# Block 0 of layer one in fp32, and weights converted in pieces of twice the width: a Trainium2 attention and two-layer kernel

## The chip, the core and the metric

The kernel runs on one core of a Trainium2 chip. The metric is device time in microseconds (us) of one execution. The core's engines work side by side, each through its own instructions in a fixed order: TensorE (PE) multiplies, VectorE (DVE) and ScalarE (ACT) work element by element, SyncE (SP) issues DMA transfers, GpSimd (POOL) does little here. An instruction starts when the semaphores that it waits for allow it; what stands behind it on its engine waits too.

## The reference

Three stages follow each other. The inputs q, k, v, M_prev, z_prev, beta and the first layer's w_in are drawn eight times larger than the drawing functions show.

```python
# B, H, S, D = 4, 8, 576, 64
scores = where(causal, -1e9, q @ k.T / sqrt(D))
a = exp(scores - max); a /= sum + 1e-9
local = a @ v
q_p = phi(q)                              # elu(q) + 1
mem = (q_p @ M_prev) / (q_p . z_prev + 1e-6)
x = g * mem + (1 - g) * local             # g = sigmoid(beta); x is 2304 x 512
h = x @ moe_w_in;  x = softplus(h) @ moe_w_out      # 512 -> 2048 -> 512
h = x @ moe2_w_in; out = relu(h) ** 2 @ moe2_w_out  # 512 -> 2048 -> 512
```

The weights arrive as 64-bit floats.

## The kernel before

**Attention** goes through 18 groups of 128 rows; nine blocks of 256 rows (two groups each) are what the layers work on. A step is one head or a few heads of a group: scores on PE, the masked maximum on DVE (line 315), the exponential on ACT (319), a split of P into two fp16 parts (331, 332), its transposition by DMA on SP (196), the product with V (355), and at a group's half and end the normalisation (374, 381) and the split and transposition of x (385 to 387). The first two groups are transposed on PE and copied by ACT (203).

**Numbers.** A product of nearly fp32 accuracy is made of three 16-bit products: each factor is split into a high and a low part, and high x high, high x low and low x high are added. In layer one these are lines 434 to 436 (h, 256 columns), 451 to 453 (output x) and 496 to 498 (the same, accumulated by quarters).

**Weights.** A piece of the first layer's weights, 128 x 4 x 128 elements of 64 bits (512 KB), is loaded through SP into one of three staging buffers (`wst`, lines 398 and 401). DVE turns its bits into fp32 with three operations (417 to 419), ACT copies the high part (421), DVE subtracts for the low part (422). There are 32 pieces: 16 of W1, 16 of W2.

**Layer one** consists of units: `h` (two of 16 column chunks of a block, then softplus on ACT, 438 to 440, DVE 441, and the split of g, ACT 444 and DVE 445), `x` (half the output columns of a block) and, for block 0, `xq` (a quarter of the sum over 2048, accumulated in PSUM over all of `xq`'s four calls). The second layer follows when all attention is done.

**Order.** A planner written out in Python emits attention steps and, between them, the units of a queue. Up to the step that completes block 0's input, W1R pieces of weights are emitted for each step. From there the queue holds, four times: eight pieces, two `h` units, one `xq` unit. FR says what share of the queue's estimated time is spread over the steps that complete block 1. A scheduler then orders each engine's instructions by emission and by priority: attention's scores have 100, weight conversions 2000 (`HW`), so conversions are taken long before their place in the emission. At `kb == 1` a passage interleaves an early part of block 1 (lines 649 to 668).

Of the kernel before, what the change touches and what calls it, by code (L numbers as in the profile page):

```python
# [8 lines left out]
F32 = mybir.dt.float32  # L9
F16 = mybir.dt.float16  # L10
# [7 lines left out]
P = 128  # L18
# [3 lines left out]
FR = 0.4  # L22
W1R = 1
B1Q = 3
# [14 lines left out]
NST = 3  # L39
# [6 lines left out]
ST2 = 4  # L46


@with_exitstack
def kernel(  # L50
# [61 lines left out]
    W1 = [w1p.tile([P, NCC, DFF], t, name=f"W1{i}") for i, t in enumerate((F16, BF16))]  # L112
    W2 = [w1p.tile([P, NFC, DM], t, name=f"W2{i}") for i, t in enumerate((F16, BF16))]
# [28 lines left out]
    make_identity(nc, ident)  # L142
    dve.memset(zero, 0.0)
# [222 lines left out]
    def emit_x(g, a):  # L366
# [15 lines left out]
        if a == 0:  # L382
            return
        xn = att.tile([P, 2, H, D], F16, name="xn")
# [21 lines left out]

    def split_piece(i, t, Ws, pool_):
# [7 lines left out]
        w = t.bitcast(I32).rearrange("p (n two) -> p n two", two=2)  # L415
        u = pool_.tile([P, 512], I32, tag="wcv", name="wcv", bufs=WCB)
# [6 lines left out]

    g_t = {}

    def unit_h(kb, fp):
        ps = mm.tile([P, 2, NB], F32, tag="mm", name="hps")
        x = x_at(kb)
        for i in range(2):
# [10 lines left out]
        act.activation(a, a, AF.Ln, bias=one[:, 0:1])  # L440
        dve.scalar_tensor_tensor(a, ps, 0.0, a, ALU.max, ALU.add)  # L441
        g = [w1p.tile([P, 2, NB], F16, name=f"g{t}_{fp}") for t in range(2)]
# [4 lines left out]
    def mm_x(ps, kb, c, f0, f1):  # L447
        for f in range(f0, f1):
            gh, gl = (t[:, f % 2] for t in g_t[kb, f // 2])
            wh, wl = (w[:, f, c * P:(c + 1) * P] for w in W2)  # L450
# [34 lines left out]
    def unit_xq(kb, q):  # L485
        if q == 0:
            for i in range(2):
                t = xac.tile([P, 2, 256], F32, name=f"xacc{i}")
                pe.matmul(t, zero, g_t[kb, 0][0], start=True, stop=False)
                xacc.append(t)  # L490
        for c in range(NCC):
            ps = xacc[c // 2][:, c % 2]
            for f in range(4 * q, 4 * q + 4):
                gh, gl = (t[:, f % 2] for t in g_t[kb, f // 2])
                wh, wl = (w[:, f, c * P:(c + 1) * P] for w in W2)
# [20 lines left out]
    order = [i for a in range(4) for i in [4 * a + t for t in range(4)] + [NPC + 4 * t + a for t in range(4)]]  # L516
# [487 lines left out]
```

## Time and profile before

| | |
|---|---|
| median of 3 runs | 960.42 us (958.69 to 961.71) |
| the profiled execution's own time | 961.28 us |
| its span in the trace | 959.5 us |
| PE busy | 878.4 us, 92% |
| DVE busy | 738.2 us, 77% |
| ACT busy | 615.6 us, 64% |

Busy PE is taken from matmul records whose ends are modelled and overlap, so it isn't PE at its peak. [...]

### The profile page before, as it was taken

What the parts mean: (1) busy time and instruction counts of PE and PEld (TensorE: products, weight loads), DVE (VectorE), ACT (ScalarE), POOL (GpSimd) and SP (SyncE); (2) the same over time, 40 slices, a digit from 0 to 9 for tenths busy, and PEclk for the clock granted to TensorE, in tenths of its full rate; (3) what the DMA queues carried; (4) which work ended last, traced back from release to release, by engine and by line L of the source; (5) the groups of instructions that cost most, each with busy time, mean ns of one, the idle gap of its engine ahead of it and who ended that gap; (6) DMA issues with size and microseconds to landing.
All of it is one profiled execution on the core that took longest, in us unless ns stands there. A gap on an engine that the chain in (4) does not pass through costs nothing.

```text
span 959.5 us, 24660 instructions
## 1 busy us (share of the span) xinstructions
PE 878.4 (92%) x10372; PEld 729.9 (76%) x10380; DVE 738.2 (77%) x1490; ACT 615.6 (64%) x1144; POOL 2.2 (0%) x10
## 2 busy tenths in 40 slices
PE   4436799899999899999999999999999999999998
PEld 3225688788878788898887888544595999999993
DVE  7997999777747766586846589999999998867640
ACT  8865878778758787796947547563357655544630
POOL 0000000000000000000000000000000000000000
PEclk8555899999999999999999999999999999999999
DMA  9999978677679996767754385630000000000001
GB/s 236 220 244 215 233 158 154 114 119 104 111 109 175 171 155 100 111 109 126 112 82 85 49 250 158 197 107 12 33 3 23 2 23 2 24 24 2 24 13 33
DMA packets 285024, 101.25 MB, mean 106 GB/s; under 512 B 248048, under 2 KB 284400, under 8 KB 284912
## 3 DMA queue, kind: packets, MB, share of 16 engines
q1 hardware_dynamic: 284672, 99.65, 53.1%
q8 instruction: 81, 1.33, 0.6%
q14 instruction: 31, 0.25, 0.1%
q10 hardware_dynamic: 240, 0.02, 0.0%
HBM read 48.78 MB, written 4.72 MB: 56 GB/s over the span
## 4 chain that ended last, share of the span: by engine, by line
PE 60%; DMA 16%; DVE 12%; ACT 6%; issue 3%; SPq 1%; DVEq 0%; ACTq 0%
DMA PT<-p 9%; PE h2ps L811 5%; PE h2ps L809 5%; PE h2ps L810 5%; PE ops L870 3%; PE ops L869 3%; PE ops L871 3%; PE hps L435 3%; PE hps L436 3%; PE hps L434 3%; PE s_ps L310 3%; DMA rawv<-in_v_dram 3%; PE pvt L355 3%; PE xps L452 2%; PE xps L453 2%
## 5 line engine op out<-in xcount | busy, mean ns | idle before, releaser
L434 PE MATMUL hps<-x,W 128*128 128x256 f16 x576 | 158.1, 276 | 3.0 <-DVE cc L276 2.2
L436 PE MATMUL hps<-x,W 128*128 128x256 f16 x576 | 158.6, 276 | 0.0
L435 PE MATMUL hps<-x,W 128*128 128x256 f16 x576 | 158.5, 276 | 0.1
L452 PE MATMUL xps<-g,W 128*128 128x256 f16 x512 | 139.3, 274 | 1.8 <-DVE g L445 1.7
L451 PE MATMUL xps<-g,W 128*128 128x256 f16 x512 | 138.2, 274 | 1.5 <-ACT g L444 1.4
L453 PE MATMUL xps<-g,W 128*128 128x256 f16 x512 | 139.3, 274 | 0.0
L319 ACT ACTIVATE Pt<-Pt,cs 128x128 f32<-128x128 f32 (+4 forms) x144 | 84.1, 584 | 51.9 <-DVE cs L315 51.6
L310 PE MATMUL s_ps<-KT,qT 128*128 128x128 f16 (+2 forms) x992 | 82.5, 225 | 31.2 <-DVE cs L315 30.7
L332 DVE TENSOR_TENSOR p<-Pt,p 128x512 f16<-128x512 f32 (+2 forms) x104 | 69.3, 666 | 34.4 <-ACT p L331 34.1
L310 PEld LDWEIGHTS <-qT 128*128 128x128 f16 (+1 forms) x992 | 58.3, 105 | 42.7 <-issue 37.5
L315 DVE CUSTOM_DVE_ANT_0 Pt<-s_ps,mask 128x128 f32<-128x128 f32 (+3 forms) x128 | 62.0, 484 | 22.8 <-PE s_ps L310 22.7
L355 PE MATMUL pvt<-V,PT 128*128 128x64 f16 (+1 forms) x1392 | 60.0, 197 | 16.6 <-DMA PT<-p 15.0
L355 PEld LDWEIGHTS <-PT 128*128 128x128 f16 (+1 forms) x1392 | 50.2, 104 | 25.9 <-DMA PT<-p 22.0
L331 ACT ACTIVATE p<-Pt 128x512 f16<-128x512 f32 (+2 forms) x104 | 63.1, 606 | 10.6 <-DMA PT<-p 9.4
L435 PEld LDWEIGHTS <-W 128*128 128x128 f16 x576 | 57.0, 99 | 10.1 <-issue 3.4
L436 PEld LDWEIGHTS <-W 128*128 128x128 bf16 x576 | 56.9, 99 | 7.1 <-issue 0.2
L434 PEld LDWEIGHTS <-W 128*128 128x128 f16 x576 | 57.0, 99 | 6.8
L421 ACT ACTIVATE W<-wcv 128x512 f16<-128x512 f32 x64 | 40.0, 625 | 30.6 <-DVE wcv L419 30.3
L453 PEld LDWEIGHTS <-W 128*128 128x128 bf16 x512 | 50.4, 98 | 8.2 <-issue 2.5
L445 DVE TENSOR_TENSOR g<-spa,g 128x512 f16<-128x512 f32 x72 | 49.4, 686 | 9.1 <-ACT g L444 8.7
L451 PEld LDWEIGHTS <-W 128*128 128x128 f16 x512 | 50.3, 98 | 7.6 <-issue 1.7
L441 DVE SCALAR_TENSOR_TENSOR spa<-hps,spa 128x512 f32<-128x512 f32 x72 | 49.4, 686 | 8.3 <-ACT spa L440 7.9
(230 smaller groups left out, 2554.6 us busy)
## 6 DMA issues: line engine op xcount, KB each, us to landing
wst<-in_moe_w_in_dram SPq DMA_DIRECT2D x32, 512.0 KB, 4.5
wst<-in_moe_w_out_dram SPq DMA_DIRECT2D x32, 512.0 KB, 4.6
rawk<-in_k_dram SPq DMA_DIRECT2D x16, 256.0 KB, 4.7
rawq<-in_q_dram SPq DMA_DIRECT2D x16, 256.0 KB, 4.5
rawv<-in_v_dram SPq DMA_DIRECT2D x16, 256.0 KB, 4.7
out_dram<-T SPq DMA_DIRECT2D x12, 256.0 KB, 2.5
PT<-p SPq DMA_TRANSPOSE x100, 3.4
mraw<-in_M_prev_dram SPq DMA_DIRECT2D x8, 128.0 KB, 4.1
```

What stands on the lines that cost most here:

```text
L310: pe.matmul(o[x * n:(x + 1) * n], qT[g][:, t * H + h, x * n:(x + 1) * n], KT[kb][:, h, a - j * P:e - j * P], start=(t == 0), stop=(t == 1),)
L315: dve.tensor_tensor_reduce(out=pw, in0=view, in1=mw, scale=-0.125, scalar=3.0e38, op0=ALU.add, op1=ALU.min, accum_out=cs[:, 0, h:h + 1],)
L319: act.activation(pf, pf, AF.Exp, bias=cs[:, 0, h:h + 1], scale=-1.0, accum_out=cs[:, 1, h:h + 1],)
L331: act.activation(v16[:, :, 0], p, AF.Copy)
L332: dve.tensor_tensor(v16[:, :, 1], p, v16[:, :, 0], ALU.subtract)
L355: pe.matmul(o[r], t[:, o0 + i + y, r], V[kb][:, z, h, :], start=(i == 0 and y + z == 0), stop=(i == nb - 1 and y > 0),)
L434: pe.matmul(o, wh, x[:, c], start=(c == 0), stop=False)
L435: pe.matmul(o, wh, x[:, NCC + c], start=False, stop=False)
L436: pe.matmul(o, wl, x[:, c], start=False, stop=(c == NCC - 1))
L451: pe.matmul(ps, wh, gh, start=(f == f0), stop=False)
L452: pe.matmul(ps, wh, gl, start=False, stop=False)
L453: pe.matmul(ps, wl, gh, start=False, stop=(f == f1 - 1))
```

## The change

Block 0 goes through layer one with fp32 operands and one product where three 16-bit ones were. Its input is transposed as fp32 on PE and copied once; its g stays fp32. The weights come in 16 pairs of pieces (1 MB, rows of 2 KB), through two staging buffers in place of three. The three bit operations write fp32 weights into slot n + 1 of one tile; after block 0's units of a group are emitted, a new unit `c` forms the high and low part of pair n in slot n, over the fp32 weights of the pair before. Block 1 accumulates by quarters as block 0 does, and the passage for its early part is gone. FR goes from 0.4 to 0.7, W1R from 1 piece to half a pair for a step. The second layer's weights keep their path.

```diff
-FR = 0.4
-W1R = 1
+FR = 0.7
+W1R = 0.5
...
-NST = 3
+NST = 2
...
+NF = 1
+HC = 0
...
-    W1 = [w1p.tile([P, NCC, DFF], t, name=f"W1{i}") for i, t in enumerate((F16, BF16))]
-    W2 = [w1p.tile([P, NFC, DM], t, name=f"W2{i}") for i, t in enumerate((F16, BF16))]
+
+    slots = w1p.tile([P, NFC + 1, 1024], F32, name="W12")
...
+        if kb < NF:
+            ps = mm.tile([P, NCC, P], F32, tag="mm", name="tps")
+            xf = xf.rearrange("p h d -> p (h d)")
+            for c in range(NCC):
+                pe.transpose(ps[:, c], xf[:, c * P:(c + 1) * P], ident32)
+            act.activation(x2_at(kb)[:, off // P::2], ps, AF.Copy)
+            return
         xn = att.tile([P, 2, H, D], F16, name="xn")
...
+    def load_pair(i):
+        t = stage.tile([P, 1024], I64, name="wst")
+        o = t.rearrange("p (a b) -> p a b", a=4)
+        if i < NPC // 2:
+            src = moe_w_in[:, 2 * i * P:2 * (i + 1) * P].rearrange("(c p) f -> p c f", p=P)
...
+        sp.dma_start(out=o, in_=src)
+        return t
...
+    def slot32(n):
+        n, o = divmod(n, 2)
+        return slots[:, n + 1].rearrange("p (a b) -> p a b", a=4)[:, :, o * P:(o + 1) * P]
+
+    def split_slot(n):
+        u = slots[:, n + 1]
+        t = slots[:, n].bitcast(F16).rearrange("p (t a) -> p t a", t=2)
+        hi, lo = t[:, 0], t[:, 1].bitcast(BF16)
+        act.activation(hi, u, AF.Copy)
+        dve.tensor_tensor(lo, u, hi, ALU.subtract)
...
             for c in range(NCC):
-                wh, wl = (w[:, c, f * P:(f + 1) * P] for w in W1)
+                if kb < NF:
+                    pe.matmul(
+                        o.rearrange("p (j t) -> p j t", j=2), slot32(pos[f])[:, c], x32[:, 2 * c:2 * c + 2],
+                        start=(c == 0), stop=(c == NCC - 1),
+                    )
+                    continue
+                wh, wl = (w[:, c] for w in slot(pos[f]))
...
+        if kb < NF:
+            g_t[kb, fp] = w1p.tile([P, 2, NB], F32, name=f"g0_{fp}")
+            dve.scalar_tensor_tensor(g_t[kb, fp], ps, 0.0, a, ALU.max, ALU.add)
+            return
...
+                if kb < NF:
+                    m = pe.matmul(
+                        ps, slot32(n)[:, f % 4], g_t[kb, f // 2][:, f % 2],
+                        start=False, stop=(f == NFC - 1 and c % 2 == 1),
+                    )
+                    continue
...
-            return 1700.0 if u[0] == "w" else 0.0
-        nmm = {"h": 24, "xq": 48, "x": 96 if len(u) == 3 else 48}[u[0]]
+        if u[0] in ("w", "c", "close"):
+            return {"w": 3000.0, "c": 0.0, "close": 0.0}[u[0]]
+        nmm = {"h": 24 if u[1] >= NF else 32, "xq": 48 if u[1] >= NF else 64, "x": 96 if len(u) == 3 else 48}[u[0]]
...
+        elif u[0] == "c":
+            with tc.high_priority(HC):
+                split_slot(u[1])
...
             with tc.high_priority(HW):
-                split_piece(order[i], pieces.pop(i), (W1, W2), stage)
-            if i + NST < 2 * NPC:
-                pieces[i + NST] = load_piece(order[i + NST], (moe_w_in, moe_w_out), sp, stage)
+                bits(pieces.pop(i), slots[:, i + 1].bitcast(I32))
+            if i + NST < NPC:
+                pieces[i + NST] = load_pair(order[i + NST])
...
-        queue += [("w", i) for i in range(max(nw, 8 * a), 8 * a + 8)]
+        queue += [("w", i) for i in range(max(nw, 4 * a), 4 * a + 4)]
         queue += [("h", 0, f) for f in range(2 * a, 2 * a + 2)] + [("xq", 0, a)]
+        if NF == 1:
+            queue += [("c", i) for i in range(4 * a, 4 * a + 4)]
...
+            for a in range(4):
+                queue += new[2 * a:2 * a + 2] + [("xq", 1, a)]
+                queue += [("c", i) for i in range(4 * a, 4 * a + 4) if NF == 2]
+            queue.append(("close",))
+            continue
```

## Rows read from the trace of the kernel before

**Rows 1.** The page's busy line, and two lines of its 40 slices.
```profile
PE 878.4 (92%) x10372; PEld 729.9 (76%) x10380; DVE 738.2 (77%) x1490; ACT 615.6 (64%) x1144; POOL 2.2 (0%) x10
...
PE   4436799899999899999999999999999999999998
...
PEclk8555899999999999999999999999999999999999
```
**Rows 2.** Windows: stretch, length, busy PE, PEld, DVE, ACT, POOL, clock, DMA share, GB/s.
```profile
11.00:85.00 74.00, 32.36 (x349) 24.26 (x344) 69.81 (x181) 55.28 (x126) 0.00 (x0) 0.54 1.15 235
85.00:120.00 35.00, 29.03 (x305) 23.58 (x306) 29.68 (x70) 24.64 (x49) 0.00 (x0) 0.79 1.14 231
120.00:185.00 65.00, 63.27 (x749) 57.22 (x748) 57.67 (x130) 49.56 (x104) 0.00 (x0) 1.00 0.73 142
185.00:222.00 37.00, 31.15 (x410) 27.24 (x408) 27.95 (x60) 28.06 (x57) 0.00 (x0) 0.95 0.78 120
222.00:300.00 78.00, 75.35 (x1127) 64.54 (x1125) 50.80 (x109) 58.84 (x118) 0.00 (x0) 1.00 0.76 122
```
**Rows 3.** Timeline of DVE: start and duration in us, then the instruction.
```profile
40.82 0.68 DVE L418 SCALAR_TENSOR_TENSOR wcv<-wst,wcv 128x512 int32<-128x512 int32 x1
41.42 0.68 DVE L221 TENSOR_TENSOR qn<-rawq,qn 128x512 f16<-128x512 f32 x1
42.02 0.42 DVE L417 TENSOR_SCALAR wcv<-wst 128x512 int32<-128x512 int32 x1
42.36 0.28 DVE L315 CUSTOM_DVE_ANT_0 Pt<-s_ps,mask 128x128 f32<-128x128 f32 x1
```
**Rows 4.** Windows of line 422 (two rows), then of line 417 (one).
```profile
11.00:84.20 73.20, 10.28 (x15) 0.55 1.15 236
84.20:185.00 100.80, 11.55 (x17) 0.92 0.87 173
...
11.00:84.20 73.20, 6.74 (x16) 0.55 1.15 236
```
**Rows 5.** Chain of work, 83 to 100 us; instructions of tile hps, first and last start.
```profile
84.25 0.68 DVE xn L386
...
L434 PE MATMUL hps<-x,W x576: 269/273/421, 87.2 to 583.9; 128*128 128x256 f16 x192
```
**Rows 6.** Windows of tile hps in a full stretch: PE, DVE, ACT.
```profile
563.00:584.00 21.00, 20.75 (x191) 3.41 (x5) 3.57 (x6) 1.00 0.60 182
```
**Rows 7.** PE's groups by line and shape, 87 to 222 us.
```profile
L434 PE MATMUL hps<-x,W 128*128 128x256 f16 x144 | 41.2, 286 | 3.0 <-DVE cc L276 2.2 <-ACT x L203 0.8
...
L498 PE MATMUL xacc<-g,W 128*128 128x256 f16 x64 | 18.6, 293 | 0.0
...
L453 PE MATMUL xps<-g,W 128*128 128x256 f16 x64 | 17.2, 273 | 0.0
...
L310 PE MATMUL s_ps<-KT,qT 128*128 128x128 f16 x184 | 16.0, 224 | 1.1 <-DVE cs L315 1.1
L355 PE MATMUL pvt<-V,PT 128*128 128x64 f16 x312 | 14.4, 195 | 7.9 <-DMA PT<-p 7.9
L347 PE MATMUL pvt<-Mt,phiT 128*128 128x64 f16 x72 | 8.1, 195 | 0.0
```
**Rows 8.** Timeline of SP's DMA queue: start, duration of the issue.
```profile
65.78 0.51 SPq L401 DMA_DIRECT2D wst<-in_moe_w_out_dram  x1
66.81 0.37 SPq L180 DMA_DIRECT2D rawq<-in_q_dram  x1
...
67.91 4.01 SPq L196 DMA_TRANSPOSE KT<-kn  x1
```
**Rows 9.** Waits, 85 to 222 us: total us, times, longest us.
```profile
PE pvt L355 <- DMA PT<-p: 7.9, 6, 2.5
ACT spa L438 <- PE hps L436: 7.6, 5, 2.9
```
**Rows 10.** A line of the page's costliest groups: PE's weight loads.
```profile
L453 PEld LDWEIGHTS <-W 128*128 128x128 bf16 x512 | 50.4, 98 | 8.2 <-issue 2.5
```

More of the change, by code (lines that the diff above doesn't have):

```diff
@@ L142 @@
     make_identity(nc, ident)
+    ident32 = stage.tile([P, P], F32, name="ident32", bufs=1)
+    make_identity(nc, ident32)
     dve.memset(zero, 0.0)
@@ L440, in unit_h @@
         act.activation(a, a, AF.Ln, bias=one[:, 0:1])
+        if kb < NF:
+            g_t[kb, fp] = w1p.tile([P, 2, NB], F32, name=f"g0_{fp}")
+            dve.scalar_tensor_tensor(g_t[kb, fp], ps, 0.0, a, ALU.max, ALU.add)
+            return
         dve.scalar_tensor_tensor(a, ps, 0.0, a, ALU.max, ALU.add)
-        g = [w1p.tile([P, 2, NB], F16, name=f"g{t}_{fp}") for t in range(2)]
+        t = w1p.tile([P, 2, NB], F32, name=f"g0_{fp}")
+        t = t.rearrange("p a b -> p (a b)").bitcast(F16).rearrange("p (t a b) -> p t a b", t=2, a=2)
+        g = [t[:, 0], t[:, 1]]
         g_t[kb, fp] = g
@@ L448, in mm_x @@
         for f in range(f0, f1):
+            n = pos[NPC + 4 * c + f // 4]
+            if kb < NF:
+                pe.matmul(ps, slot32(n)[:, f % 4], g_t[kb, f // 2][:, f % 2], start=(f == f0), stop=(f == f1 - 1))
+                continue
             gh, gl = (t[:, f % 2] for t in g_t[kb, f // 2])
-            wh, wl = (w[:, f, c * P:(c + 1) * P] for w in W2)
+            wh, wl = (w[:, f % 4] for w in slot(n))
             pe.matmul(ps, wh, gh, start=(f == f0), stop=False)
@@ L488, in unit_xq @@
                 t = xac.tile([P, 2, 256], F32, name=f"xacc{i}")
-                pe.matmul(t, zero, g_t[kb, 0][0], start=True, stop=False)
-                xacc.append(t)
+                pe.matmul(t, zero, mask[:, 0], start=True, stop=False)
+                xacc[i:i + 1] = [t]
         for c in range(NCC):
@@ L515 @@
     pieces = {}
-    order = [i for a in range(4) for i in [4 * a + t for t in range(4)] + [NPC + 4 * t + a for t in range(4)]]
+    order = [i for a in range(4) for i in [2 * a + t for t in range(2)] + [NPC // 2 + 4 * t + a for t in range(2)]]
+    for n, i in enumerate(order):
+        for o in range(2):
+            c, g = divmod(i - NPC // 2, 4)
+            pos[2 * i + o if i < NPC // 2 else NPC + 4 * (2 * c + o) + g] = 2 * n + o
     steps = [(g, h) for g in range(NC) for h in range(0, H, GRP[g])]
@@ L544 @@
     for i in range(NST):
-        pieces[i] = load_piece(order[i], (moe_w_in, moe_w_out), sp, stage)
+        pieces[i] = load_pair(order[i])
     prep_m(0)
@@ L619 @@
         s += 1
-        while nw < 2 * NPC and nw < W1R * s:
+        while nw < NPC and nw < W1R * s:
             run_unit(("w", nw))
@@ L648 @@
         if kb == 1:
-            done = 4 - sum(u[0] == "xq" for u in queue)
-            if done < 4:
-                at = 0
-                while done < B1Q:
-                    done += queue[at][0] == "xq"
-                    at += 1
-                nh = 2 * done
-                early = new[:nh] + [("x", kb, c, 0, 2 * nh) for c in range(NCC // 2)]
-                out_q = queue[:at]
-                for u in queue[at:]:
-                    if u[0] != "w" and early:
-                        out_q += early
-                        early = []
-                    out_q.append(u)
-                    if u[0] == "w" and early:
-                        out_q.append(early.pop(0))
-                queue = out_q + early + [("close",)]
-                if done < 4:
-                    new = new[nh:]
-                    xs = [("x", kb, c, 2 * nh, NFC) for c in range(NCC // 2)]
-            else:
-                queue.append(("close",))
+            for a in range(4):
+                queue += new[2 * a:2 * a + 2] + [("xq", 1, a)]
+                queue += [("c", i) for i in range(4 * a, 4 * a + 4) if NF == 2]
+            queue.append(("close",))
+            continue
         queue += new + xs
```

24 lines of the change are left out of this document (18 added, 6 removed).

## The prediction

> **What bounds the kernel now.** I read the page's busy line first: PE is busy 92% of the span, so what PE does not do in time is lost. The slices then say where it is not busy: its digits are 3 to 7 in the first five slices (120 us), and the granted clock is half in the second to fourth [rows 1]. The windows give the same in microseconds [rows 2]: from 11 to 85 us DVE is busy 69.8 of 74 us and PE 32.4, at a granted clock of 0.54; from 120 us on PE is busy 63.3 of 65, while DVE is still at 57.7; from 185 to 222 PE sinks to 31.2 of 37; later it is full. So the start is bound by DVE, the rest by PE, and the 961.28 us are PE's work plus what PE misses, most of it before 120 us.
>
> How fast DVE really goes is seen in its timeline, not in durations: neighbouring starts [rows 3] lie 0.60 us apart for a 512-wide fp32 or int32 operation of two inputs (40.82 to 41.42) and 0.34 us for the one-input shift (42.02 to 42.36), though they last 0.68 and 0.42. A weight piece costs DVE 0.34 + 3 x 0.60 = 2.14 us. Up to 84.2 us 16 pieces were begun and 15 ended [rows 4]: 16 x 1.54 + 15 x 0.60 = 34 us of DVE. The last DVE step of block 0's input is at 84.25 us, its first product of layer one at 87.2 us [rows 5].
>
> How much PE has to do: in a full stretch at full clock 191 products of 256 columns took 21 us [rows 6], 0.11 us each; I scale with columns (0.055 for 128, 0.027 for 64). From 87 to 222 us, about when block 1 has left layer one, there are 144 products on each of three h lines and 64 on each of three lines for block 0's and again for block 1's second half, together 816 of 256 columns, 184 of 128, 384 of 64 and a few tiny ones [rows 7]: 89.8 + 10.1 + 10.4 + 2 = 112 us of work in 135 us. PE misses 23 us there.
>
> **The change, part by part.** The sum is made against the profiled execution, 961.28 us, which lies 0.86 above the median of 960.42; the span is 959.5 and 1.8 lie around it.
>
> (1) Work taken from DVE before block 0 is ready. The subtraction for the second part of the weights goes behind block 0: 15 x 0.60 = 9.0 us. The two input splits of block 0 go: 1.2 us. Pieces twice as wide: a start-to-start time of 0.60 is 512 columns and a rest; the shift's 0.34 at the same rest fits 0.27 + 0.07, so 0.07 is saved for each operation merged, 0.2 us for each pair, 1.6 us for eight pairs. Together 11.8 us. From above, then, block 0 is ready 12 us earlier; from below not at all, or somewhat later, since nothing but two staging buffers holds the conversions back. I take 8, two thirds, because DVE was 94% busy there and SP is nearly as full: its DMA instructions of 57 to 72 us follow each other almost without a gap, transposes taking up to 4.0 us [rows 8], and halving the number of weight loads frees only about 0.5 us each, eight times. What is next late is those transposes and loads.
>
> [...]
>
> (2) PE's added work. Block 0 loses 384 products of 0.11 us (42.2 us) and gets 128 in fp32. No row of this kernel shows an fp32 product. From below: it costs what one 256-column product costs, 128 x 0.11 = 14 us, a gain of 28. From above: twice four of them (four at the half clock that this stretch partly has), 113 us, a loss of 70. I take four, 0.44 us: a factor with twice the digits is two halves, two such factors make four products of halves, and the kernel's own scheme leaves out the fourth. That is 56.3 us, +14. The eight opening and input transposes for block 0 become eight fp32 ones, under 1 us either way.
>
> [...]
>
> (3) What PE misses between block 0's start and 222 us. Before, a group of eight pieces asks 8 x 2.14 = 17.1 us of DVE for 96 products, 10.6 us of PE: block 0 waits for DVE. After, the group's four pairs ask 4 x 2.87 = 11.5 us of DVE for 32 fp32 products, 14 us of PE: DVE can feed it. Its total work in the stretch hardly changes: 17 pieces [rows 4] at 2.14 were 36.4 us; eight pairs of bits at 2.87 and 16 wide subtractions at 1.13 are 41.1, less eight g subtractions and two additions of partial sums (10 x 0.60). PE's work is 126 us against some 113 of DVE. Bounds: all 23 us are recovered, or none. PE's largest wait there is for the transposes of P, 7.9 us in six waits [rows 9], and it stays. I take 10.
>
> (4) Added waits. Each split of a pair writes over the fp32 weights of the pair ahead, so the copy on ACT waits for block 0's products on them. Queued behind it on ACT are the exponentials of later attention steps and the next softplus; DVE's p split and PE's score products wait for those. In emission order the splits stand behind the unit that they wait for, so I price this at 0, covered by PE's distance from ACT; without that cover it is the second rival. Block 1's first accumulation must wait until block 0's sums have left PSUM (four operations of about 0.6 us, 2.4 us); two h units of block 1 (48 products, 5 us) stand between, and if they don't cover it the scores behind it on PE wait those 2.4 us. The first two loads are 1 MB instead of three of 512 KB; M's second load is queued behind them on SP, 0.5 MB later, about 2 us at the 235 GB/s of that stretch [rows 2], and not needed before block 0's second step. ACT loses eight g copies and merges 32 weight copies to 16; it is not the bound (55.3 of 74 us).
>
> (5) FR and W1R shift units against attention steps; total work is unchanged, and their worth is in (1) and (3).
>
> Sum: 961.28 - 8 + 14 - 10 = 957.3, and 0.86 less for the median: 956.5 us. Nothing behind 222 us changes.
>
> **Rivals.**
> A, the start gives more: the full 11.8 us, and PE misses only 6 us of the 23. 961.28 - 12 + 14 - 17 - 0.86 = 945.5. For it: DVE at 94%. Against: SP's fullness.
>
> B, slower: the early places that DVE gets free are filled by conversions. They have priority 2000, and the two staging buffers hold four pieces' worth where three held three. From three more pairs (8.6 us) ahead of block 0's input the gain of (1) is gone; PE's 14 us stay, and 4 of (3) come back: 961.28 + 14 - 4 - 0.86 = 970.5. For it: 16 pieces had been begun by 84 us [rows 4], twice the eight that the emission order has put out by the step that completes block 0's input. Against: a pair holds its buffer longer (1 MB to land, 2.87 us of DVE where 1.54 was), so by 75 us again about eight pairs are through.
>
> C, slower: the copies of the splits stand too early in ACT's order and ACT waits for fp32 products. Four groups; a wait up to half an accumulation unit (16 x 0.44 = 7 us), so 4 x 3.5 = 14 us on the forecast: 970.5. Against: ACT's softplus waits for h products here already, 7.6 us in five waits [rows 9], and PE is full all the same.
>
> D, fp32 isn't what it says: one pass each. 956.5 - 42 = 914.5. The output's accuracy would suffer, which speaks against it.
>
> E, fp32 weight loads are not hidden. A load now takes 0.098 us and lies beside a product [rows 10]; four for each fp32 product, 512, exposed: +50 us, 1006.5. Against: today's loads are as many per product as there would be passes.
>
> F, the gains of (1) and (3) just pay for (2): about 960.
>
> **How the numbers follow.** The forecast of 956.5 gets 0.43, with a range of its own of 946 to 965 (start 4 to 12 us earlier, 5 to 14 us recovered); A 0.16, B 0.17, C 0.10, D 0.03, E 0.04, F 0.07. A measurement tells 0.3%, 2.9 us, from no change. Of the forecast's 0.43 about 0.29 lie under 957.5, 0.10 within, 0.04 above. Faster: 0.29 + 0.16 + 0.03 = 0.48; same 0.10 + 0.07 = 0.17; slower 0.04 + 0.17 + 0.10 + 0.04 = 0.35. The range takes in A and the slower rivals B and C with some 4 us beyond each: 941 to 975, leaving D, E and a little of each edge outside. The far bounds of (2) are D, E and the half clock; only D and E have a mechanism here.
>
> **What would show it.** (1): the first fp32 h product at 75 to 83 us instead of 87.2; at 85 or later B is right. Bits about 2.87 us a pair in starts. (2): 128 fp32 products (or their passes) that occupy 0.44 us each in a full stretch. (3): block 1's last sums before 222 us, and PE's busy share from 120 to 185 still near 97%. (4): ACT idle before the weight copies, released by PE's fp32 lines, would be C. All stretches behind layer one's block 2 should be alike but for a shift; if not, the change has reached further than I see, and the prediction is wrong for a reason not listed.

## The result, and the profile after

The changed kernel takes 975.81 us (median of four, 970.98 to 976.14) where the kernel before takes 961.07 beside it: 1.0131 times, 95% interval 1.0096 to 1.0166. It is 14.7 us slower; 956.5 was forecast, and 975.81 lies just outside the range that ended at 975. The profiled execution took 975.52 us with a span of 973.7.

The page of the changed kernel, the busy line and two lines of slices, against [rows 1]:

```profile
PE 893.7 (92%) x10246; PEld 742.4 (76%) x10246; DVE 730.4 (75%) x1414; ACT 608.3 (62%) x1116; POOL 2.6 (0%) x12
...
PE   3549599899999899999899999999999999999998
...
PEclk9999789999999999999999999999999999999999
```

PE is as busy as before in share, 92%, in a span that is 14 us longer: 893.7 us where 878.4 were. Of the slices (24 us each) the fourth, from 73 us, is 9 where 6 was, and the fifth is 5 where 7 was.

The windows of the same five stretches as [rows 2] (stretch, length, busy PE, PEld, DVE, ACT, POOL, granted clock as a share of full speed, DMA share, GB/s):

```profile
11.00:85.00 74.00, 43.13 (x412) 33.46 (x412) 66.63 (x151) 51.89 (x115) 0.00 (x0) 1.00 1.09 251
85.00:120.00 35.00, 25.72 (x177) 20.98 (x175) 29.88 (x52) 18.44 (x38) 0.00 (x0) 0.80 1.06 236
120.00:185.00 65.00, 60.14 (x549) 52.70 (x550) 49.70 (x96) 46.81 (x90) 0.00 (x0) 0.95 0.59 115
185.00:222.00 37.00, 33.25 (x442) 29.36 (x441) 24.42 (x56) 27.62 (x58) 0.00 (x0) 1.00 0.68 115
222.00:300.00 78.00, 73.15 (x1085) 61.55 (x1082) 49.38 (x104) 54.49 (x107) 0.00 (x0) 1.00 0.77 118
```

PE gains 10.8 us of busy time up to 85 us (43.1 for 32.4), at a full clock, and loses 3.3 from 85 to 120 at the same granted clock of 0.8 that it had before. From 222 to 300 us it is idle 4.9 us where it was idle 2.7. DVE does less in every stretch but the second, and that bought nothing.

**What PE did, stage by stage.** At a granted clock of 0.50 a product takes about twice as long (in the trace of the kernel before, products of 256 columns start 0.213 us apart from 87.6 to 92.2 us, at a clock of 0.50, and 0.109 apart from 94.1 to 96.5 us, at 1.00), so busy time is no measure of work. I count PE's work by its products instead, at their spacing at the full clock: 0.109 us for one of 256 columns, 0.056 for 128 and 0.029 for 64 or fewer (medians of lines 310 and 355 in the kernel before), 0.216 for each of the two records of an fp32 one (shown below). What is left of a stretch is missed: idle time, and what the lower clock cost. All counts are made in the same way from each kernel's trace:

| missed by PE, us | 0–75 | 75–100 | 100–140 | 140–222 | 222–300 | 300–600 | sum to 600 |
|---|---|---|---|---|---|---|---|
| before | 61.3 | 14.3 | 6.7 | 10.2 | 2.1 | 17.0 | 111.7 |
| after | 58.3 | 3.9 | 17.7 | 7.2 | 7.1 | 16.4 | 110.6 |
| e1_own_x | 58.8 | 1.5 | 7.9 | 12.6 | 4.4 | 20.7 | 105.8 |
| e2_wide_only | 61.8 | 22.1 | 13.8 | 4.8 | 8.9 | 19.5 | 130.9 |
| e3_one_pass | 58.8 | 13.8 | 28.7 | 13.5 | 2.8 | 26.1 | 143.7 |
| e5_quarters | 61.0 | 14.0 | 11.6 | 7.8 | 5.8 | 19.3 | 119.4 |
| e12_narrow_own | 58.4 | 6.0 | 7.0 | 8.7 | 5.6 | 20.2 | 105.9 |
| e15_after_one_bit_op | 48.6 | 13.0 | 16.8 | 7.4 | 3.7 | 15.1 | 104.7 |
| e16_before_one_bit_op | 57.6 | 6.4 | 13.7 | 16.8 | 5.3 | 22.6 | 122.5 |
| e18_fp32_only | 59.0 | 12.4 | 12.6 | 10.3 | 4.5 | 18.1 | 116.9 |

The first two rows account for the result. Up to 100 us the changed kernel misses 13.4 us less, the earlier start. Between 100 and 140 it misses 11.0 more, between 222 and 300 another 5.0, and by 600 us the two have missed the same. PE's work has grown by some 13 us, and nothing pays for it. Up to 222 us the two miss 92.5 and 87.1 us: 5.4 are recovered where the forecast had 18 in its steps (1) and (3). Of the 17.7 us between 100 and 140 PE is idle in 10.9 (29.08 of 40 us busy), and the rest goes to the clock, 0.74 there; in the kernel before it is idle in 2.8 of the 6.7, at 0.92.

The fp32 products of the h units (line 479: duration min/median/max in ns, first and last start, shape):

```profile
L479 PEld LDWEIGHTS hps<-x,W x128: 190/190/337, 74.5 to 153.2; 128*128 128x128 f32 x128
...
L479 PE MATMUL hps<-x,W x128: 379/379/792, 74.6 to 153.4; 128*128 128x256 f32 x128
```

And eight records in a full stretch (start, duration in us):

```profile
77.68 1.89 PE L479 MATMUL hps<-x,W 128*128 128x256 f32 x8
```

The first product starts at 74.6 us where the first of block 0 stood at 87.2 [rows 5]. There are 64 products in this line and 128 records, so each is two records. Eight records take 1.89 us, the last of them 0.379, so starts are (1.89 - 0.379) / 7 = 0.216 us apart and a product costs 0.43. The weight load of 0.190 fits under a record.

The hole, PE's timeline between 98 and 111 us (start, duration, instruction, idle time before it and what ended it), and PE's waits from 85 to 140 us (total, times, longest):

```profile
101.34 0.37 PE L359 MATMUL pvt<-V,PT 128*128 128x64 f16 x6 [2.06 <-DMA PT<-p]
...
105.69 0.80 PE L314 MATMUL s_ps<-KT,qT 128*128 128x128 f16 x6 [3.13 <-DVE cs L319]
109.69 1.22 PE L479 MATMUL hps<-x,W 128*128 128x256 f32 x2 [3.20 <-DMA x<-xn]
```

```profile
PE pvt L359 <- DMA PT<-p: 5.8, 3, 3.2
PE hps L479 <- DMA x<-xn: 3.2, 1, 3.2
PE s_ps L314 <- DVE cs L319: 3.1, 1, 3.1
```

In these 12 us PE waits three times for more than 2 us: for transposes of P, for DVE's score maximum, and then, in block 0's fourth h unit, for a transpose into x. That last wait is one that the forecast did not have. Block 0's fp32 input lies in the same tile as block 1's 16-bit input, in columns that interleave, and the product waits for block 1's first half, which block 0 does not need.

### The profile page after: what moved, and what is told of

The parts are those of the page before. It is cut to its first block, busy times and chain, and to the rows that moved or that the text cites. A ratio compares the mean times of both kernels' runs of the same rounds, so it can differ in the third digit from the quotient of the medians.

```text
span 973.7 us, 24248 instructions
## 1 busy us (share of the span) xinstructions
PE 893.7 (92%) x10246; PEld 742.4 (76%) x10246; DVE 730.4 (75%) x1414; ACT 608.3 (62%) x1116; POOL 2.6 (0%) x12
## 4 chain that ended last, share of the span: by engine, by line
PE 64%; DMA 18%; DVE 8%; ACT 6%; issue 3%; SPq 1%; ACTq 0%; DVEq 0%
DMA PT<-p 9%; PE h2ps L869 5%; PE h2ps L870 4%; PE h2ps L871 4%; PE ops L929 3%; PE ops L931 3%; PE ops L930 3%; PE xps L512 3%; PE xps L513 3%; PE xps L514 3%; PE pvt L359 3%; PE s_ps L314 3%; DMA rawq<-in_q_dram 3%; PE hps L487 3%; PE hps L486 3%
## 5 line engine op out<-in xcount | busy, mean ns | idle before, releaser
L486 PE MATMUL hps<-x,W 128*128 128x256 f16 x512 | 139.4, 273 | 0.1
L487 PE MATMUL hps<-x,W 128*128 128x256 f16 x512 | 139.3, 273 | 0.0
L485 PE MATMUL hps<-x,W 128*128 128x256 f16 x512 | 138.7, 273 | 0.0
L323 ACT ACTIVATE Pt<-Pt,cs 128x128 f32<-128x128 f32 (+4 forms) x144 | 84.0, 584 | 63.3 <-DVE cs L319 63.0
L513 PE MATMUL xps<-g,W 128*128 128x256 f16 x448 | 121.3, 273 | 1.1 <-DVE g L502 1.1
L514 PE MATMUL xps<-g,W 128*128 128x256 f16 x448 | 121.5, 273 | 0.0
L512 PE MATMUL xps<-g,W 128*128 128x256 f16 x448 | 120.3, 273 | 0.3 <-ACT g L501 0.3
L314 PE MATMUL s_ps<-KT,qT 128*128 128x128 f16 (+2 forms) x992 | 87.0, 226 | 29.6 <-DVE cs L319 28.8
L314 PEld LDWEIGHTS <-qT 128*128 128x128 f16 (+1 forms) x992 | 60.4, 105 | 43.4 <-issue 35.7
L486 PEld LDWEIGHTS <-W 128*128 128x128 f16 x512 | 50.1, 98 | 5.8
L485 PEld LDWEIGHTS <-W 128*128 128x128 f16 x512 | 50.1, 98 | 5.7
L487 PEld LDWEIGHTS <-W 128*128 128x128 bf16 x512 | 50.1, 98 | 5.6
L496 DVE SCALAR_TENSOR_TENSOR spa<-hps,spa 128x512 f32<-128x512 f32 x64 | 44.0, 687 | 12.1 <-ACT spa L491 12.0
L491 ACT ACTIVATE spa<-spa,one 128x512 f32<-128x512 f32 x72 | 51.4, 714 | 0.8
L502 DVE TENSOR_TENSOR g<-spa,g 128x512 f16<-128x512 f32 x64 | 44.0, 688 | 10.3 <-ACT g L501 10.2
L489 ACT ACTIVATE spa<-hps 128x512 f32<-128x512 f32 x72 | 42.1, 584 | 14.7 <-PE hps L487 8.5
L514 PEld LDWEIGHTS <-W 128*128 128x128 bf16 x448 | 43.8, 98 | 6.0 <-issue 1.3
```

The lines of the kernel that those rows point to most:

```text
L314: pe.matmul(o[x * n:(x + 1) * n], qT[g][:, t * H + h, x * n:(x + 1) * n], KT[kb][:, h, a - j * P:e - j * P], start=(t == 0), stop=(t == 1),)
L323: act.activation(pf, pf, AF.Exp, bias=cs[:, 0, h:h + 1], scale=-1.0, accum_out=cs[:, 1, h:h + 1],)
L485: pe.matmul(o, wh, x[:, c], start=(c == 0), stop=False)
L486: pe.matmul(o, wh, x[:, NCC + c], start=False, stop=False)
L487: pe.matmul(o, wl, x[:, c], start=False, stop=(c == NCC - 1))
L512: pe.matmul(ps, wh, gh, start=(f == f0), stop=False)
```

## The experiments

Ratios are against the kernel before, run beside each (median 960.7 to 962.3). Several of these kernels spread by 5 to 12 us from execution to execution (e5_quarters 973 to 983, e15 970 to 980, e16 962 to 975), so a profile can lie some us off its median: e16's is the slowest of its ten executions (974.8, median 968.3), e5's and e15's are the fastest of their four (973.0 for 979.4, 969.9 for 977.5). Differences of 3 us between them are not read as more than that.

### Four parts of the change

**e1_own_x**: the shared tile undone.

```diff
-            act.activation(x2_at(kb)[:, off // P::2], ps, AF.Copy)
+            act.activation(x2_at(3)[:, off // P::2], ps, AF.Copy)
...
-        x32 = x2_at(kb)
+        x32 = x2_at(3)
```

> The changed kernel, with block 0's fp32 input laid into a part of another x tile that is not in use yet, so that block 1's transposes of x no longer share it. Theory W (a shared tile): in the changed kernel the fourth h unit of block 0 starts at 109.7 us, released by the transpose of block 1's x, and TensorE misses 18 us between 99 and 132 us; without the shared tile that unit starts before 102 us, the clock is not halved for so long, and the time falls by 8 to 14 us, to 962 to 968. Rival V (weights late): pairs 10 to 15 leave the bit operations only at 95 to 139 us and block 0 waits for them; the unit may start earlier, but the end moves by less than 3 us (973 to 979). Rival P (the fp32 products themselves): the 13 us of added products are the loss; less than 3 us as well.

973.47 us, 1.0130 [1.0101, 1.0159]. Its windows from 85 us:

```profile
85.00:120.00 35.00, 32.05 (x233) 27.40 (x232) 29.97 (x50) 20.29 (x38) 0.00 (x0) 1.00 1.10 237
120.00:185.00 65.00, 61.35 (x637) 54.16 (x637) 53.82 (x110) 52.38 (x103) 0.00 (x0) 0.97 0.64 124
185.00:222.00 37.00, 31.84 (x373) 27.38 (x372) 23.15 (x51) 24.95 (x50) 0.00 (x0) 0.86 0.74 116
222.00:300.00 78.00, 74.66 (x1114) 64.04 (x1112) 51.31 (x108) 58.72 (x116) 0.00 (x0) 0.98 0.76 123
```

The hole closes: 32.05 of 35 us busy at a full clock where 25.72 at 0.80 were, and the fourth h unit starts at 90.4 us instead of 109.7. The end hardly follows, by 2.3 us of median and 4.1 of span; the ratio to before is 1.0130 where it was 1.0131, so no gain is clear of the noise. By the table 9.8 us come back between 100 and 140, and 5.4 of them go between 140 and 222, 4.3 between 300 and 600.

**e2_wide_only**: no fp32; each pair is split right behind its bits. What is left is the wide pieces, the slots, block 1 by quarters and FR 0.7.

```diff
-NF = 1
+NF = 0
...
                 bits(pieces.pop(i), slots[:, i + 1].bitcast(I32))
+                split_slot(i)
```

> The changed kernel without fp32: block 0 goes through layer one with three 16-bit products as the other blocks do, and each pair's two parts are formed right behind its bits. Wide pieces, two buffers, the slots and block 1 by quarters stay. Theories W and P: with fp32 its cost goes; the wide pieces are a small gain or nothing, 957 to 963. Rival Q (the wide pieces with two buffers, or the lost early passage of block 1, cost by themselves): 968 or more.

981.6 us, 1.0214 [1.0187, 1.0242]. The rest of the change costs 20 us without fp32, and fp32 takes 6 of them back. This kernel also starts late: its first h product stands at 109.1 us, 22 later than before, and between 85 and 140 us PE waits 10.8 us for DVE's score maxima. Why, and how much of the 20 us that is, stays open; e6b_wide below, also with the split right behind the bits, starts at 81.6.

**e3_one_pass**: the fp32 products read the upper 16 bits of both operands, one 16-bit product in place of an fp32 one; part of the precision is left out.

```diff
-        x32 = x2_at(kb)
+        x32 = x_t[0].bitcast(BF16)[:, :, 1:NB:2]
```

(and the same view for the weights and g).

> The changed kernel with each of block 0's fp32 products made on the upper 16 bits of both factors alone; the lower halves are left out, all else (waits, order of the units, sharing of the tile) stays. It takes some 41 us (55 less 14) of work from TensorE. Theory P (TensorE's added work is the loss): 975.8 less 30 to 41, 935 to 946. Theory W or V (waits, not work): less than half of it is got back, 956 to 972.

968.2 us, 1.0065 [1.004, 1.009]. 41 us of work are gone (an estimate from the spacings above: 128 products at 0.109 us where 0.43 was), 7.6 us of time. Two windows:

```profile
85.00:120.00 35.00, 19.02 (x191) 14.25 (x191) 29.38 (x56) 22.14 (x45) 0.00 (x0) 0.74 1.10 237
120.00:185.00 65.00, 52.50 (x629) 46.00 (x627) 56.56 (x110) 52.14 (x103) 0.00 (x0) 0.90 0.74 134
```

PE is idle 16.0 and 12.5 us where the changed kernel is idle 9.3 and 4.9; the table has 143.7 missed for 110.6. In this stretch PE's work was not what set the time. The order moved too, though it was meant to stay: the fourth h unit starts at 85.9 us where it stood at 109.7, and doesn't wait for block 1's transpose.

**e4_fr04**: FR back to 0.4 in the changed kernel.

```diff
-FR = 0.7
+FR = 0.4
```

> The changed kernel with FR back at 0.4: fewer of block 0's units are emitted between the steps that complete block 1, more behind. Theory W: units of block 0 that share the tile stand behind more of block 1's transposes, and TensorE misses more before 135 us: 977 to 990. Rival R (0.7 puts units in TensorE's order before their weights are there, and attention waits behind them): faster than the changed kernel by 3 us or more, 965 to 973.

987.08 us, 1.0275 [1.0239, 1.0311]. FR 0.7 is worth 11 us here.

### The same parts on the kernel before

**e5_quarters**: block 1 by quarters, its early passage gone.

```diff
-            done = 4 - sum(u[0] == "xq" for u in queue)
...
+            for a in range(4):
+                queue += new[2 * a:2 * a + 2] + [("xq", 1, a)]
+            queue.append(("close",))
+            continue
```

> The kernel before with one edit: block 1 goes through layer one by quarters behind block 0, and the early passage of its first twelve tiles, interleaved with the last eight weight pieces, is gone; no fp32, narrow pieces, three buffers, FR 0.4. Theory Q (losing the early passage is what cost e2_wide_only its 20 us): 10 to 20 us above before, ratio 1.010 to 1.021, and PE idle between 100 and 140 us rises from about 6 us to 12 or more. Theory S (the wide pieces in two buffers are what cost it): within 3 us of before, ratio 0.997 to 1.003.

979.43 us, 1.0183 [1.0135, 1.023]; the profiled execution's span is 971.2. Its windows to 185 us:

```profile
11.00:85.00 74.00, 33.72 (x356) 25.39 (x356) 70.23 (x183) 56.75 (x129) 0.00 (x0) 1.00 1.16 240
85.00:120.00 35.00, 29.60 (x316) 24.29 (x316) 30.41 (x70) 23.69 (x48) 0.00 (x0) 0.90 1.12 225
120.00:185.00 65.00, 58.14 (x687) 51.48 (x686) 57.87 (x130) 47.11 (x100) 0.00 (x0) 0.95 0.73 147
```

From 120 to 185 us PE is busy 58.1 us where [rows 2] have 63.3: the last weight pieces come, and the twelve tiles of block 1 that stood beside them are missing.

**e6_wide, e6b_wide**: pieces twice as wide in two buffers. In e6_wide the one buffer for the formed weights also served W3 and W4's conversions, which had two before; e6b_wide gives it a name of its own.

```diff
-NST = 3
+NST = 2
...
+        u = stage.tile([P, 1024], I32, name="wcw", bufs=1)
...
-                split_piece(order[i], pieces.pop(i), (W1, W2), stage)
+                split_pair(order[i], pieces.pop(i))
```

> The kernel before with one edit: pieces twice as wide (bits and split on 1024 elements, 1 MB loads, two staging buffers); no fp32, the early passage of block 1 and FR 0.4 stay; the key rows of chunk 1 are loaded a little later, into another pool, to make room. Theory S (a wide piece lands late, 6.6 to 6.9 us where 4.5 were, and two buffers leave DVE without one): 10 to 20 us above before, ratio 1.010 to 1.021, first h product near 100 us where before has 87. Theory Q: within 3 us of before or up to 5 us below it, since 16 merges of four operations save some of DVE's time; first h product at 85 to 88 us.

> e6_wide again, but its single buffer for the formed fp32 weights has a name of its own, so the conversions of W3 and W4, which in e6_wide had one buffer instead of two, keep their two. Theory Q: the first h product stays at about 81 us, the last product of layer one's x lines at about 607 us as before, and now the whole is within 3 us of before, ratio 0.997 to 1.003. Theory S (the wide pieces cost time themselves): 5 us or more above before, ratio above 1.005.

e6_wide took 990.88 us (1.0312 [1.0263, 1.0361]), but its last product of the x lines stands at 607 us as before; the loss lies wholly behind layer one, in the conversions that I had not meant to touch. e6b_wide took 962.06, 1.0006 [0.9985, 1.0027], with the first h product at 81.6 us. The wide pieces are free, and a start 5.6 us earlier is worth nothing that can be measured: the first sign of what follows.

**e17_before_fr07** (FR 0.7 in the kernel before) and **e18_fp32_only** (block 0 in fp32 with slots, all else as before; the last pair's fp32 weights in a tile of their own to make room):

```diff
-FR = 0.4
+FR = 0.7
```

```diff
+    def s32(n):
+        return slots[:, n + 1] if n + 1 < NFC else wl
```

> The kernel before with one constant: FR 0.7 for 0.4, so more of block 0's layer one stands before block 1's attention steps end. If FR brings something by itself, as it brought 11 us in the changed kernel (e4_fr04): 950 to 957, ratio 0.990 to 0.997. If it only pays where block 1 has no early passage: 960 to 975, ratio 0.999 to 1.015, as fewer of block 1's tiles can run beside the last weight pieces.

> Block 0 in fp32 with slots and splits behind it, and everything else as in the kernel before: narrow pieces in three buffers, early passage of block 1, FR 0.4 (e9_early with FR back to 0.4). If fp32 costs what its products add and the start gives nothing back (the account so far): 13 to 15 us above before, 974 to 976, ratio 1.012 to 1.016, and PE misses about as much up to 222 us as before. If FR 0.7 hurts beside the early passage: below e9_early's 974.9, 962 to 970. If FR 0.4 hurts with fp32 as in e4_fr04: 980 or more.

e17 took 966.52 us, 1.0054 [1.0031, 1.0077], e18 982.17 us, 1.0209 [1.0173, 1.0246]. fp32 alone costs 20 us, more than its own 13: with FR 0.4 few of block 0's units stand early enough to use the earlier start (its third h unit begins at 107 us; in e9_early below, which differs in FR alone, at 85).

### Parts taken back from the changed kernel

**e7_narrow** (narrow pieces, three buffers), **e8_hw0** (the conversions' priority 2000 becomes 0), **e9_early** (e7 with the early passage of block 1 put back), **e10_early_own** (e9 with e1's edit), **e12_narrow_own** (e7 with e1's edit). The edits are those shown above, taken back or joined; e8 is one line:

```diff
-HW = 2000
+HW = 0
```

> The changed kernel with one part undone: narrow pieces again (512 elements, 512 KB loads, three buffers), written into halves of the same slots; fp32 block 0, the slots' splits, block 1 by quarters and FR 0.7 stay. Theory S: 5 to 12 us below the changed kernel's 975.8, ratio to before 1.001 to 1.008. Theory Q: within 3 us of it or slower by the merges lost (32 more starts of three operations at 0.07 us, 3 us of DVE), ratio 1.011 to 1.017.

> The changed kernel with one constant changed: the weight conversions' priority 2000 becomes 0, so a conversion no longer goes ahead of the attention steps that stand before it in emission order. Theory B (conversions pulled ahead take DVE's and the DMA queues' places from block 0's second tiles and from the transposes of P between 99 and 132 us): the fourth fp32 h unit starts before 100 us where it starts at 109.8, and the time falls by 5 to 10 us to 966 to 971. Theory W0 (conversions are what layer one waits for there, so they can only come later): the first h product moves from 74.7 to 80 us or later and the time is the same or longer, 975 to 985.

> The changed kernel with narrow pieces (as in e7_narrow) and with the early passage of block 1 put back: its first twelve tiles run beside the last weight pieces, the rest by whole sums as before; the fp32 weights of the last pair lie in a tile of their own to make room. Theory Q (the lost early passage costs 11 us or more): 8 to 14 us below e7_narrow's 972.5, 958 to 965, ratio 0.998 to 1.004. Theory V (behind fp32 the early passage has nothing to fill, since block 0's longer products already occupy PE while the pieces come): within 4 us of e7_narrow, 968 to 976, ratio 1.008 to 1.016.

> e9_early with block 0's fp32 input in a place of its own, as in e1_own_x, so the fourth h unit of block 0 waits for no column of block 1. Theory Q with W (both edits gain, each in its own stretch): 2 to 8 us below e9_early, 952 to 963, ratio 0.991 to 1.002. Rival (what is gained before 140 us is given back behind it, as in e1_own_x): within 3 us of e9_early.

> e7_narrow with block 0's fp32 input in a place of its own; block 1 by quarters stays. If the two edits add: 975.8 less 3 for the narrow pieces and 2 to 4 for the place, 968 to 971, ratio 1.007 to 1.010. If the stretch behind 140 us takes back what is gained: 971 to 974, ratio 1.010 to 1.014.

In us, with ratios: e7 972.48 (1.0119 [1.0097, 1.014]), e8 977.55 (1.0168 [1.0138, 1.0198]), e9 974.93 (1.0124 [1.0092, 1.0155]), e10 970.2 (1.0078 [1.0049, 1.0108]) and e12 970.95 (1.008 [1.0049, 1.0111]). The early passage, worth 18 us to the kernel before (e5), is worth nothing behind fp32 (e9 beside e7), as if block 0's longer products filled the time that it filled; that they do is a reading of these times. The priority of the conversions does nothing by itself (e8), and the best of the five still loses 8 us. e12 misses 7.0 us between 100 and 140 where the changed kernel misses 17.7, and 20.2 between 300 and 600 where that misses 16.4; e1 was alike. Block 2 and its followers stand at other places among the attention steps in every one of these kernels, and I have not settled why these places are worse.

### Is it the conversions or the loads?

**e16_before_one_bit_op** and **e15_after_one_bit_op** leave out two of the three bit operations of each piece of W1 and W2, 38 and 36 us of DVE. The edit of e15; e16's is the same in `split_piece`:

```diff
+        if u.shape[-1] == 1024:
+            dve.tensor_scalar(u, w[:, :, 1], 3, 0x3BFFFFFF, ALU.logical_shift_left, ALU.bitwise_and)
+            return
         dve.tensor_scalar(u, w[:, :, 1], 3, 0x3FFFFFFF, ALU.logical_shift_left, ALU.bitwise_and)
```

> The changed kernel with one of the three bit operations of each weight pair of W1 and W2, the shift; the two that set sign and low bits are left out, so the weights are wrong. DVE loses 32 operations of 1.13 us, 36 us, by about 140 us. Theory V: 10 to 25 us less than the changed kernel, 951 to 966. Theories D and O: within 5 us of it, as the loads still come at the pace of the queues.

> The kernel before with one of the three bit operations of each weight piece of W1 and W2 (the weights are wrong). DVE loses 64 operations of 0.60 us, 38 us, by about 174 us. Theory V: 5 to 15 us less than before, 946 to 956, as block 0 starts about 8 us earlier. Theories D and O: within 5 us of before.

e16 took 968.25 us, 1.006 [1.0034, 1.0087], e15 977.45 us, 1.0141 [1.0094, 1.0187]. e16 is the cleanest experiment of the study, since it gives the earlier start for nothing. The first h products of e16, then of e15:

```profile
L437 PE MATMUL hps<-x,W x576: 271/273/421, 73.7 to 597.2; 128*128 128x256 f16 x192
```

```profile
L482 PE MATMUL hps<-x,W x128: 379/379/795, 60.5 to 154.5; 128*128 128x256 f32 x128
```

13.5 us earlier than before, 14.1 earlier than the changed kernel, with nothing added, and neither is faster. e15 is less clean: its fourth h unit runs into the shared tile and starts at 110.8 us, where the changed kernel has 109.7, and PE waits there 4.0 us for the transpose into x, and 1.3 more at 140. e16 has no such wait. Its windows, the first four stretches of [rows 2]:

```profile
11.00:85.00 74.00, 42.81 (x472) 33.49 (x472) 58.92 (x169) 61.34 (x141) 0.00 (x0) 0.65 1.14 248
85.00:120.00 35.00, 27.77 (x321) 23.08 (x319) 24.40 (x56) 23.98 (x50) 0.00 (x0) 1.00 1.16 218
120.00:185.00 65.00, 54.74 (x617) 47.12 (x616) 42.22 (x98) 43.47 (x93) 0.00 (x0) 0.89 0.78 151
185.00:222.00 37.00, 30.90 (x417) 27.16 (x415) 27.19 (x59) 30.17 (x62) 0.00 (x0) 0.95 0.69 114
```

PE is busy 10.4 us more up to 85 us (at a clock of 0.65 for 0.54) and 8.5 less from 120 to 185. The idle time has moved behind the work. Where it ends is seen in the last sum of block 2's input on DVE (the second half of its second chunk), first before, then after, e15, e16:

```profile
192.12 0.42 DVE L381 TENSOR_TENSOR xf<-xt 128x256 f32<-128x256 f32 x1
```

```profile
198.48 0.42 DVE L385 TENSOR_TENSOR xf<-xt 128x256 f32<-128x256 f32 x1
```

```profile
187.83 0.42 DVE L385 TENSOR_TENSOR xf<-xt 128x256 f32<-128x256 f32 x1
```

```profile
183.75 0.42 DVE L381 TENSOR_TENSOR xf<-xt 128x256 f32<-128x256 f32 x1
```

Block 0's input is complete at 81.8, 70.9, 58.6 and 66.2 us in these four, 23 us apart; block 2's at 192.1, 198.5, 187.8 and 183.8, 15 apart and in another order. Most of the lead is gone by then. And layer one's units stand among these steps in the emission order: in e16 the first six h units of block 0 begin 12 to 19 us earlier than before (73.7 to 108.1 for 87.2 to 122.6), block 1's first six between 4.5 us earlier and 4 later (127.3 to 157.7 for 131.8 to 153.7), and block 0's last two at 168.9 and 184.7 for 166.8 and 180.6, though the last piece's subtraction now starts at 139 us and not at 178. This fits units that have their data and wait for their place in PE's order, behind an attention step that has not come. PE's waits from 100 to 222 us fit it as well, first before, then e16:

```profile
PE pvt L355 <- DMA PT<-p: 7.9, 6, 2.5
PE s_ps L310 <- DVE cs L315: 1.1, 2, 0.8
PE xps L451 <- ACT g L444: 1.1, 1, 1.1
```

```profile
PE pvt L355 <- DMA PT<-p: 10.4, 7, 3.0
PE s_ps L310 <- DVE cs L315: 5.2, 5, 1.6
PE xacc L499 <- ACT g L447: 2.5, 2, 2.2
PE pvt L347 <- DVE xt L374: 1.0, 2, 0.9
PE xacc L500 <- DVE g L448: 0.8, 1, 0.8
```

PE waits 19.9 us where it waited 10.1; 16.6 and 9.0 of them are waits of attention's products (pvt, s_ps), and none is for a weight. It is not block 2's input that holds block 2: in e16 that input is complete 8.4 us earlier than before, and block 2's first h product starts 6.7 us later (214.5 for 207.8). Why PE waits longer for attention there is not shown.

**e13_after_half_loads** and **e14_before_half_loads**: half of the weights of W1 and W2 are not loaded, the buffer before is converted again.

```diff
-                pieces[i + NST] = load_pair(order[i + NST])
+                pieces[i + NST] = t if i // NST % 2 == 0 else load_pair(order[i + NST])
```

> The changed kernel with every second weight pair of W1 and W2 not loaded: its bits are formed from the pair loaded before, so the weights are wrong and 8 MB less are read. Theory D (the DMA engines, 1.06 to 1.15 of full up to 140 us, hold the attention steps and with them the order of work on PE): 10 to 25 us less than the changed kernel, 951 to 966, and PE's waits for the transposes of P between 74 and 222 us fall from 10.4 to under 5. Theory V (DVE holds it): within 4 us of the changed kernel. Theory O (neither: the order of work on PE): within 4 us too.

> The kernel before with half of the weight pieces of W1 and W2 not loaded (formed from the piece loaded before, so the weights are wrong). Theory D: it gains less than e13 gains on the changed kernel, 0 to 10 us, 951 to 961, since its loads are spread up to 174 us. Theories V and O: within 4 us of before.

e13 took 981.04 us, 1.0189 [1.0165, 1.0213], e14 964.05 us, 1.0016 [0.9996, 1.0036]. Loads do not hold the kernel before: e14 misses 1.8 us between 100 and 140 for 6.7, and 14.8 between 140 and 222 for 10.2. e13 ran into something else:

```profile
11.00:85.00 74.00, 19.19 (x176) 13.94 (x176) 71.22 (x125) 38.62 (x83) 0.00 (x0) 1.00 0.98 213
85.00:120.00 35.00, 30.82 (x315) 26.79 (x314) 25.45 (x69) 26.98 (x60) 0.00 (x0) 0.85 0.79 132
```

With data always at hand DVE is busy 71 of 74 us, all bits are formed by 82 us instead of 139, the attention steps wait, and block 0 starts at 103 us. This fits the forecast's rival B, as if the shortage of loads had held the conversions back until it was taken away. Whether full DMA engines (share 1.0 to 1.1 up to 140 us) slow the changed kernel's attention steps stays open for that reason.

## Why the prediction was wrong

**The sum.** Two steps failed. Step (3) took 10 us of PE's missed time as recovered between block 0's start and 222 us; 2.4 were (31.2 us missed from 75 to 222 us before, 28.8 after). Step (1) took 8 us off the end for an earlier start; the start came, and what it gave was lost behind it. Without these two the sum is 961.28 + 14 - 0.86 = 974.4; measured are 975.8. That it comes so near is partly luck: PE's work isn't paid in time one for one here (41 us less of it gave 7.6 in e3, 13 less was 6 us slower in e2), and parts that the sum put at nothing cost 18 and 5 us by themselves (e5, e17). (By its own terms the forecast is 956.4, and A and B are 945.4 and 970.4; nothing hangs on these tenths.)

**Step (1), the start**, was right as an event and wrong as a gain. Block 0 starts 12.6 us earlier, above even the upper bound of 12; rival B fell here. The forecast took each microsecond that it credited off the end. e16 is the counterexample: 13.5 us earlier with nothing added, 6 us slower. What failed is that the 8 us were taken off the end. That would have needed a look at what PE waits for later: in the kernel before 9.0 of its 10.1 us of waits between 100 and 222 us are at attention's products, and with the earlier start of e16 they were 16.6.

**Wide pieces** did what the spacing of starts said. Two starts of the changed kernel's DVE:

```profile
30.59 1.22 DVE L463 SCALAR_TENSOR_TENSOR W<-wst,W 128x1024 int32<-128x1024 int32 x1
...
31.72 0.28 DVE L319 CUSTOM_DVE_ANT_0 Pt<-s_ps,mask 128x128 f32<-128x128 f32 x1
```

The bit operation of 1024 elements starts at 30.59 and the next operation at 31.72, 1.13 us apart, and two of 512 were 1.20: 0.07 saved by a merge, as [rows 3] gave. But e6b shows no worth in time (1.0006 [0.9985, 1.0027]).

**Step (2), fp32**, was right as PE's work: 256 records at 0.216 are 55.3 us against 56.3 forecast, 13 more than the 384 products that they replace. Rivals D and E fell. An fp32 product takes 0.43 us in the trace, four times 0.109 within 2%. It is two records there; that four products of halves lie behind it, the forecast's reason for the four, is not shown.

**Step (3), 10 of 23 us recovered**, failed. PE misses 28.8 us between 75 and 222 us, where 13 should have been left; 11.0 of the start's 13.4 are spent between 100 and 140. Of the signs set for it, PE's share from 120 to 185 us is 92.5% (60.14 of 65) and not 97, and block 1's last sum stands at 224.6 us and not before 222. Its premise was that block 0 waits for DVE. The trace of the kernel before has this for PE from 87 to 222 us, the window and all its waits:

```profile
87.00:222.00 135.00, 122.27 (x1450) 107.19 (x1450) 113.30 (x252) 100.33 (x207) 0.00 (x0) 0.94 0.85 158
```

```profile
PE pvt L355 <- DMA PT<-p: 7.9, 6, 2.5
PE hps L434 <- DVE cc L276: 2.2, 1, 2.2
PE s_ps L310 <- DVE cs L315: 1.1, 2, 0.8
PE xps L451 <- ACT g L444: 1.1, 1, 1.1
PE hps L434 <- ACT x L203: 0.8, 1, 0.8
```

PE is idle for 12.7 of the 23 us, and none of its waits is for a weight (the h products wait 3.0 us, for attention's `cc` on DVE and for ACT's copy of x); 7.9 are the transposes of P that the forecast itself left standing. The other 10 us or so are no idle time but products at a granted clock below 1.00 (0.94 on average). So step (3) took 10 us where some 5 of idle time were open to it. A unit that stands late in PE's order need not show a wait of its own, so the order could still carry a delay by DVE; but e16, which takes 38 us off DVE, got nothing for it. And block 1's early passage, which had filled part of this stretch, was given up; its loss has no term in the forecast's sum. On the kernel before it is worth 18 us (e5).

**Step (4), added waits at 0**: the wait that came was not among those listed. It was the shared tile of block 0's and block 1's input; closing it gives 1.5 to 4.7 us of median (e1, e12 beside e7, e10 beside e9), hardly clear of the noise. Rival C is small: ACT's splits waited for fp32 products four times, 2.7 us in all, and no wait of PE on them stands in its list.

**Step (5), no work changed and no worth outside (1) and (3)**, was wrong for FR. By itself it costs the kernel before 5 us (e17) and saves the changed one 11 (e4).

**"Nothing behind 222 us changes"** was wrong. Block 2's first h product stands at 228 us instead of 208, and the places of later blocks among the attention steps differ in every kernel here.

The parts do not add. With all medians beside the kernel before (961):

| | FR 0.4 | FR 0.7 |
|---|---|---|
| early passage | 961 | 966.5 (e17) |
| quarters | 979.4 (e5) | 981.6 (e2) |
| fp32, early passage | 982.2 (e18) | 974.9 (e9) |
| fp32, quarters | 987.1 (e4) | 975.8 (after) |

(e2, e4 and the changed kernel have wide pieces, the other cells narrow ones; e7, the last cell with narrow ones, has 972.5. e2 also has the late start.) Alone, fp32 costs 20 us, the quarters 18, FR 5, the wide pieces 0; together 15, not 43. That fp32 and the early passage fill the same idle time fits the passage's worth, 18 us without fp32 (e5) and none with it (e9 beside e7); that fp32 needs its units early fits FR's worth, 11 us in the changed kernel, 7 in e9 beside e18, and -5 in the kernel before. No version here beats the kernel before; e6b_wide equals it. Faster attention steps between 75 and 190 us would be the thing to look for, and that was not tried.

## What to carry to other kernels

Before an earlier start is taken off the end, look for what the later work of the stretch waits for, and ask whether that comes earlier too; if not, the idle time moves behind the work. An idle stretch can be filled once, so list what already fills it before a second filler is credited. Split the time that an engine misses into idle time and lower clock, and see what each wait ends on: only the waits that the change removes can be credited. Take away the suspected bottleneck outright, as the bit operations were here, before a rearrangement that relieves it is built.

## What the runs showed of the hardware

The granted clock of the first stretch differs where the work there is alike. From 11 to 85 us it is 0.54 in the profile of the kernel before [rows 2] and 1.00 in that of e5_quarters, whose edit lies behind that stretch, with 32.4 and 33.7 us of PE busy; e13 had 1.00 with 19.2. Block 0 starts at 87.2 and 86.2 us in the first two. It isn't the kernel that decides: of 62 executions of the kernel before, 17 have a mean clock of 0.949 to 0.959 over the whole run and 45 one of 0.984 to 0.998, and their medians are 962.0 and 961.5 us. So the two groups differ by 0.5 us, next to nothing for this kernel. For the others this isn't settled: e5's executions took 982.5 and 982.0 us at 0.946 and 0.953, but 973.0 and 976.9 at 0.991, and four are too few to tell.

Less work can start a stage later: e14, which drops half of the loads, starts block 0 at 90.6 us instead of 87.2. An edit can also move the order in which the engines' queues are filled, as e3's fourth h unit shows; whether that is the reason here is not shown. An experiment that takes one thing away may take an order away with it, and only effects larger than that are read here.
